# Attention and two MLPs on one core: transpositions in a PSUM bank of their own over two heads, and weight conversion without a shift

## The chip, the cores and the metric

The kernel runs on one core of one Trainium2 chip. The metric is the device time of one execution in microseconds (us), the median of several runs. TensorE (PE in the profile; PEld is its weight load), VectorE (DVE), ScalarE (ACT), GpSimd (POOL) and the queue of transfers (SP) each work through their own list of instructions in order, and wait for one another by semaphores. Matmul results land in PSUM, which has eight banks of 128 partitions x 512 float32.

## The reference, cut to what matters

```python
q, k, v: (4, 8, 576, 64) float32
q_rot, k_rot = (rotate(q), rotate(k))                 # rotary embedding over the 576 positions
scores = q_rot @ k_rot.T / sqrt(64)
attn   = exp(scores - max(scores, -1)); attn /= sum(attn, -1) + 1e-9
x      = (attn @ v) laid out as (2304 tokens, 512)
x      = (sigmoid(x @ w_gate) * (x @ w_val)) @ w_out  # 512 -> 1536 -> 512
h      = x @ w_in
out    = where(h > 0, h, exp(min(h, 0)) - 1) @ w_out2 # 512 -> 2048 -> 512
```

The weights of the MLPs are float64. Products are made at float32 accuracy from two parts, a rounded high part and the rest, so that each product is three matmuls in the MLPs and two in the scores.

## The kernel before, in words

**Attention.** There are 32 heads in 16 pairs. The work of a head is laid out in a *slot* of ten *steps* (`NSTEP`); step `h` of slot `i` issues one tile of scores of head `i` (`scores`, two matmuls K1xQ1 and K2xQ2 into a tile `s`, exponential on ACT into `e`), one tile of the row maxima of the head two slots later (`maxima`, one matmul into a tile `mt`, reduced by DVE into `MX`), and five steps late one product with V (`values`, tile `pv`). Steps 4 and 9 are the last score tile of each half, whose stationary has 64 columns instead of 128; their exponential is split in two, and DVE makes the low part `p` one and a half steps later (`low_part`). At step 0 DVE joins the maxima of the next head (`join`, `MJ`), and at step 1.5 PE turns them into a row (`max_row`, tile `mr` in the same pool as `mt`), which DVE copies (`row`) and a DMA takes into the operands `W`. An even head (the first of its pair) has ten `mt` beside it, an odd one eight.

**Preparing a pair.** POOL makes the rotary embedding of q and k (`rope_ops`; `rk`, `rt`, `rq`). `split` then transposes it on PE in four pieces, two for k and two for q (three, two, two and two 128x128 transpositions), into PSUM tiles `Tk_0`, `Tk_256`, `Tq_0`, `Tq_256`; for each piece ACT copies the rounded part into `hl` and DVE subtracts it for the rest. For pair `pr` all four pieces stand in slot `2*pr-4`, an even one, at steps 1.5 to 7.5. `move` sends the parts to `W` by DMA.

**PSUM in attention.** Eight banks: `ps_mt` has three (for `mt` and `mr`), `ps_qk` three (for `s` and for all transpositions), `ps_pv` two. A tile that finds no free bank makes PE wait for the reader of an earlier tile of its pool.

**Weights.** `split_w` converts float64 weights from their two 32-bit words, in pieces of 128x256, with seven DVE instructions (lines 121, 124, 126, 131, 134, 137, 140), one ACT copy (138) and two POOL instructions (141, 143). It is a generator; `pull` takes it one `yield` further. In attention one pull stands at step 2 and one at step 5 of each slot from 6 to 29, and each of them is one DVE instruction there. What is left of the first chunk's weights is pulled once a step from slot 30. In the MLPs the pulls are spread over the matmuls of the chunk before.

**MLPs.** Six chunks of the gated MLP and eight of the second (ELU) one, each for five blocks of up to 512 tokens; the second layer of a block runs one block behind the first. In the ELU chunks DVE also makes the activation (672, 673) and adds every output tile to `z` (730).

The order on each engine is the order in which the code is written; `at(slot, step, ...)` puts a call on an agenda that is emitted at that place.

Of the kernel before, what the change touches and what calls it, by code (L numbers as in the profile page):

```python
# [14 lines left out]
I32 = mybir.dt.int32  # L15
I64 = mybir.dt.int64


@with_exitstack
def attention_moe_moe_kernel(  # L20
# [81 lines left out]
    def split_w(c, n, half):  # L102
# [10 lines left out]
        for j in range(0, size, WP):  # L113
# [19 lines left out]

            nc.vector.tensor_single_scalar(e, low, 8, op=ALU.logical_shift_right)  # L134
            if c == 0:
                yield
            nc.vector.tensor_single_scalar(m, a.bitcast(I32), -0x00800000, op=ALU.bitwise_and)  # L137
            nc.scalar.copy(h, a)  # L138
            yield
            nc.vector.scalar_tensor_tensor(mf, in0=e, scalar=2.0**-44, in1=mf, op0=ALU.mult, op1=ALU.mult)  # L140
            nc.gpsimd.tensor_tensor(out=a, in0=a, in1=h.bitcast(F32), op=ALU.subtract)  # L141
# [44 lines left out]
    with ExitStack() as att:  # L186
# [9 lines left out]
        rope_p = prep.enter_context(tc.tile_pool(name="rope", bufs=1))  # L196
        ps_mt = banks.enter_context(tc.tile_pool(name="ps_mt", bufs=3, space=bass.MemoryType.PSUM))
        ps_qk = banks.enter_context(tc.tile_pool(name="ps_qk", bufs=3, space=bass.MemoryType.PSUM))
        ps_pv = banks.enter_context(tc.tile_pool(name="ps_pv", bufs=2, space=bass.MemoryType.PSUM))

# [119 lines left out]

        def split(pr, which, half, later=None):
# [6 lines left out]
            T = ps_qk.tile([P, 512], F32, tag="qk", name=f"T{which}{pr}_{c0}")[:, 0:n]  # L328
            rows = [rot[pr, which][:, c // P] for c in range(c0, c0 + HM, P)] + ([rot[pr, "t"]] if tails else [])
            for j, r in enumerate(rows):  # L330
                nc.tensor.transpose(T[:, j * P : (j + 1) * P], r.rearrange("p h d -> p (h d)"), ident)
            c0 += 0 if which == "k" else S + TL
            hi, lo = (parts[pr][:, 2 * j : 2 * j + 2].rearrange("p w s -> p (w s)")[:, c0 : c0 + n] for j in range(2))
            nc.scalar.copy(hi, T)
            rest = lambda: nc.vector.tensor_tensor(out=lo, in0=T, in1=hi.bitcast(F32), op=ALU.subtract)
            if later is None:
                rest()
            else:
                at(*later, rest)

# [82 lines left out]
        def scores(i, h):  # L423

            a, t = divmod(h, ST + 1)
            n = P if t < ST else TL
            if t == ST:

                p = probs[i, h] = p_p.tile([P, HA], F32R, tag="pt", name=f"p{i}_{h}")[:, 0:HS]
            else:  # L430
                e = probs[i, h] = e_p.tile([P, HA], F32, tag="ef", name=f"e{i}_{h}", bufs=2 * ST)[:, 0:HS]
            s = ps_qk.tile([P, 512], F32, tag="qk", name=f"s{i}_{h}")[0:n, 0:HS]
            for st, mv in (("K1", "Q1"), ("K2", "Q2")):
                nc.tensor.matmul(  # L434
                    s, lhsT=operand(i, st, t * P, n), rhs=operand(i, mv, a * HS, HS), start=st == "K1", stop=st == "K2"
                )
# [11 lines left out]
        def values(i, h):  # L448
# [9 lines left out]
            e = probs.pop((i, h))  # L458
            if t == ST:
                nc.tensor.matmul(out_ps[0:D], lhsT=VT[par][:, ab, 0:D], rhs=e, start=False, stop=False)  # L460
                nc.tensor.matmul(out_ps, lhsT=VT[par][:, ab, D : 3 * D], rhs=e, start=False, stop=True)
# [76 lines left out]
        for which in "kq":  # L538
            for half in range(2):
                at(-5, 1, split, 0, which, half)  # L540
            at(-5, 1, copies, 0, which, nc.vector.tensor_copy)
# [3 lines left out]
        for (which, half), st in zip((("k", 0), ("k", 1), ("q", 0), ("q", 1)), (10, 11, 17, 18)):  # L545
            at(-2, st, split, 1, which, half)
        at(-2, 13, copies, 1, "k", nc.scalar.copy)
# [3 lines left out]
        for pr in range(NPAIR):  # L551
            s0 = 2 * pr
            if pr > 1:
# [10 lines left out]
                for j, (which, half) in enumerate((("k", 0), ("k", 1), ("q", 0), ("q", 1))):  # L564
                    at(s0 - 4, (6.5, 7.5, 8.5, 9.5)[j] if pr == 2 else (1.5, 3.5, 5.5, 7.5)[j], split, pr, which, half, None if pr == 2 else (s0 - 4, 2.5 + 2 * j))
                at(s0 - 4, 10 if pr == 2 else 9, move, pr, 0)
                at(s0 - 4, 10 if pr == 2 else 9, last_queries, pr, nc.gpsimd.tensor_copy)
                at(s0 - 4, 19, move, pr, 1)
# [25 lines left out]
        at(5, 0, pull, gen)  # L594
        pulls = 14 * len(halves(0)) + 1
        early = [(slot, step) for slot in range(6, NHEAD - 2) for step in (2, 5)]
# [209 lines left out]
```

## Time and profile before

| what | us |
|---|---|
| median of 3 runs (lowest, highest) | 1164.22 (1162.93, 1165.01) |
| span of the profiled execution | 1164.2 |
| first score matmul of head 0 | 24.2 |
| first matmul of the first MLP | 319.7 |
| first matmul of the second MLP | 766.1 |
| end of the last matmul | 1159.6 |
| PE busy / DVE busy / POOL busy / ACT busy | 1138.5 / 937.7 / 605.0 / 451.2 |

The profile is that of one execution; its span and the median of the runs agree, so sums against the span are sums against the median. A *head* below is the stretch from one head's first score matmul to the next head's. PE is busy nearly all of the time, by a record in which the ends of pipelined matmuls are modelled, so what PE loses is read from the lengths of equal pieces of work (heads, chunks) and from the starts of matmuls, and not from the busy share. Instructions on DVE also overlap by a little: the next one starts before the row of the last one has ended.

### The profile page before, as it was taken

The page shows a single profiled execution, that of the slowest core. Times are in us where ns is not written, and L with a number is a line of the kernel's source. Part 1 is how long each engine was busy: PE and PEld are TensorE (multiplying, and loading weights), DVE is VectorE, ACT ScalarE, POOL GpSimd, SP SyncE. Part 2 cuts the span into 40 slices and gives each one's busy share as a digit, 9 for nine tenths or more (in the row PEclk, how much of TensorE's full clock was granted, in tenths as well). Part 3 has the DMA queues.
Part 4 walks back from the last instruction along what each step waited for, and adds up shares of the span by engine and source line. Part 5 has one row for each costly group of instructions (what it writes and reads, how often), then busy time and mean ns, then how long its engine had stood idle before and what let it go on. Part 6 is the DMA issues. An engine that isn't in the chain of part 4 may idle for free.

```text
span 1164.2 us, 16786 instructions
## 1 busy us (share of the span) xinstructions
PE 1138.5 (98%) x5728; PEld 960.5 (82%) x5728; DVE 937.7 (81%) x1994; ACT 451.2 (39%) x1037; POOL 605.0 (52%) x695
## 2 busy tenths in 40 slices
PE   5999999999999999999999999999999999999998
PEld 3888888888888888888888888888888888888887
DVE  6768888887876888667777766888999999999844
ACT  4666666667753321221222122344322222222221
POOL 8766666863343554434444435775554545545521
PEclk9999999999999999999999999999999999999999
DMA  6667677767121211111111110111111111110004
GB/s 166 158 161 184 163 179 169 163 158 160 41 94 37 73 55 40 52 37 47 44 38 54 37 55 19 37 37 37 55 37 55 37 37 55 37 55 1 1 37 127
DMA packets 58757, 88.03 MB, mean 76 GB/s; under 512 B 18176, under 2 KB 30736, under 8 KB 58672
## 3 DMA queue, kind: packets, MB, share of 16 engines
q1 hardware_dynamic: 58672, 86.96, 28.2%
q8 instruction: 45, 0.74, 0.3%
q14 instruction: 40, 0.33, 0.1%
HBM read 55.45 MB, written 4.87 MB: 52 GB/s over the span
## 4 chain that ended last, share of the span: by engine, by line
PE 78%; DVE 17%; ACT 2%; issue 1%; DMA 1%; SPq 0%; POOL 0%; POOLq 0%
PE h L647 12%; PE h L648 12%; PE h L649 12%; PE pv L463 9%; PE o L647 7%; PE o L648 7%; PE o L649 7%; PE s L434 7%; DVE z L730 3%; PE mt L387 3%; DVE g L673 2%; DVE g L672 2%; DVE ca L131 2%; DVE cm L140 1%; DVE MX L389 1%; DVE ce L134 1%
## 5 line engine op out<-in xcount | busy, mean ns | idle before, releaser
L679 POOL TENSOR_TENSOR gl<-g,gh 128x512 fp32r<-128x512 f32 (+1 forms) x140 | 168.6, 1204 | 330.2 <-ACT gh L678 261.7
L678 ACT CAST gh<-g 128x512 fp32r<-128x512 f32 (+1 forms) x140 | 81.0, 579 | 308.2 <-DVE g L673 171.1
L434 PE MATMUL s<-W 128*128 128x288 f32 (+1 forms) x640 | 182.0, 366 | 3.8 <-DVE p L444 1.3
L648 PE MATMUL h<-xl,wh 128*128 128x512 f32 (+1 forms) x480 | 176.6, 368 | 0.0
L647 PE MATMUL h<-xh,wh 128*128 128x512 f32 (+1 forms) x480 | 176.6, 368 | 0.0
L649 PE MATMUL h<-xh,wl 128*128 128x512 f32 (+1 forms) x480 | 176.5, 368 | 0.0
L463 PE MATMUL pv<-e,VF 128*128 128x288 f32 x512 | 166.0, 407 | 0.0
L141 POOL TENSOR_TENSOR ca<-ca,wh 128x256 f32<-128x256 f32 x136 | 111.5, 820 | 96.8 <-DVE cm L137 82.4
L389 DVE TENSOR_REDUCE MX<-mt 128x1 f32<-128x288 f32 x288 | 127.5, 450 | 40.9 <-PE mt L387 38.7
L434 PEld LDWEIGHTS s<-W 128*128 128x128 f32 (+1 forms) x640 | 106.1, 182 | 32.1 <-DVE p L444 5.2
L138 ACT CAST wh<-ca 128x256 fp32r<-128x256 f32 x136 | 55.1, 405 | 195.0 <-DVE ca L131 195.0
L143 POOL TENSOR_TENSOR wl<-ca,cm 128x256 fp32r<-128x256 f32 x136 | 111.0, 816 | 18.5 <-DVE cm L140 12.1
L441 ACT ACTIVATE e<-s 128x288 f32<-128x288 f32 x256 | 104.3, 411 | 41.4 <-PE s L434 38.2
L648 PE MATMUL h<-yl,wh 128*128 128x512 f32 (+1 forms) x320 | 117.7, 368 | 0.0
L649 PE MATMUL h<-yh,wl 128*128 128x512 f32 (+1 forms) x320 | 117.7, 368 | 0.0
L647 PE MATMUL h<-yh,wh 128*128 128x512 f32 (+1 forms) x320 | 117.7, 368 | 0.0
L668 DVE TENSOR_TENSOR g<-h,g 128x512 f32<-128x512 f32 (+1 forms) x60 | 38.2, 637 | 95.1 <-PE h L649 92.3
L647 PE MATMUL o<-wh,gh 128*128 128x512 f32 x288 | 112.7, 391 | 1.5 <-DVE z L730 1.2
L648 PE MATMUL o<-wl,gh 128*128 128x512 f32 x288 | 112.2, 389 | 0.0
L649 PE MATMUL o<-wh,gl 128*128 128x512 f32 x288 | 112.1, 389 | 0.0
L649 PEld LDWEIGHTS h<-xh,wl 128*128 128x128 f32 x480 | 90.5, 189 | 15.1
L647 PEld LDWEIGHTS h<-xh,wh 128*128 128x128 f32 x480 | 90.5, 189 | 15.0
(110 smaller groups left out, 2514.4 us busy)
## 6 DMA issues: line engine op xcount, KB each, us to landing
W<-hl SPq DMA_DIRECT2D x90, 288.0 KB
raw<-in_moe_w_out_dram SPq DMA_DIRECT2D x28, 512.0 KB
raw<-in_moe_w_in_dram SPq DMA_DIRECT2D x16, 512.0 KB
raw<-in_moe_w_gate_dram SPq DMA_DIRECT2D x12, 512.0 KB
raw<-in_moe_w_val_dram SPq DMA_DIRECT2D x12, 512.0 KB
rb<-d SPq DMA_DIRECT2D x32, 144.0 KB
k<-in_k_dram SPq DMA_DIRECT2D x16, 256.0 KB
q<-in_q_dram SPq DMA_DIRECT2D x16, 256.0 KB
```

The source lines that it names most:

```text
L138: nc.scalar.copy(h, a)
L141: nc.gpsimd.tensor_tensor(out=a, in0=a, in1=h.bitcast(F32), op=ALU.subtract)
L143: nc.gpsimd.tensor_tensor(out=l, in0=a, in1=mf, op=ALU.add)
L389: nc.vector.tensor_reduce(out=MX[pr % 2][:, a, c : c + 1], in_=m, axis=AX.X, op=ALU.max, negate=True)
L434: nc.tensor.matmul(s, lhsT=operand(i, st, t * P, n), rhs=operand(i, mv, a * HS, HS), start=st == "K1", stop=st == "K2")
L441: nc.scalar.activation(e, s, AF.Exp, scale=SCALE)
L463: nc.tensor.matmul(out_ps, lhsT=VF[par][:, ab, t], rhs=e, start=t == 0, stop=False)
L647: nc.tensor.matmul(ps, lhsT=ah, rhs=bh, start=j == 0, stop=False)
L648: nc.tensor.matmul(ps, lhsT=ah, rhs=bl, start=False, stop=False)
L649: nc.tensor.matmul(ps, lhsT=al, rhs=bh, start=False, stop=j == n - 1)
L678: nc.scalar.copy(hi, g)
L679: nc.gpsimd.tensor_tensor(out=lo, in0=g, in1=hi.bitcast(F32), op=ALU.subtract)
```

## The change

**Banks.** `ps_mt` has two banks instead of three. The freed bank is a pool `ps_t` for transpositions. For the first four pairs only the last piece of q of pairs 0 and 1 uses it; the rest stays in `ps_qk` as before.

**Order from the fifth pair on (`pr` >= 4).** The two k pieces move to slot `2*pr-5`, an odd one, and the two q pieces stay in slot `2*pr-4`; each is at step 4 or step 9, all in `ps_t`. The transpositions are no longer issued in a row: they are put on a list `between`, and `one_between` takes one of them ahead of each of the two score matmuls of that step (and the third of `Tk_256` ahead of the value product). The ACT copy follows behind the step, and DVE's subtraction one and a half steps behind it, except for `Tq_256`, where it follows at once. `move` and `last_queries` go from step 9 to step 10.

**Weights.** The shift of the low word by 8 bits (line 134 before) is gone; the last DVE instruction reads the low word itself as an unsigned number and multiplies by 2^-52 instead of 2^-44. For the first chunk each piece has six pulls instead of seven, so 12 fewer are left for slot 30 and later.

```diff
-            nc.vector.tensor_single_scalar(e, low, 8, op=ALU.logical_shift_right)
-            if c == 0:
-                yield
             nc.vector.tensor_single_scalar(m, a.bitcast(I32), -0x00800000, op=ALU.bitwise_and)
             nc.scalar.copy(h, a)
             yield
-            nc.vector.scalar_tensor_tensor(mf, in0=e, scalar=2.0**-44, in1=mf, op0=ALU.mult, op1=ALU.mult)
+            nc.vector.scalar_tensor_tensor(
+                mf, in0=low.bitcast(U32), scalar=2.0**-52, in1=mf, op0=ALU.mult, op1=ALU.mult
+            )
...
-        ps_mt = banks.enter_context(tc.tile_pool(name="ps_mt", bufs=3, space=bass.MemoryType.PSUM))
+        ps_mt = banks.enter_context(tc.tile_pool(name="ps_mt", bufs=2, space=bass.MemoryType.PSUM))
         ps_qk = banks.enter_context(tc.tile_pool(name="ps_qk", bufs=3, space=bass.MemoryType.PSUM))
+        ps_t = banks.enter_context(tc.tile_pool(name="ps_t", bufs=1, space=bass.MemoryType.PSUM))
...
+            for j, r in enumerate(rows):
+                if apart:
+                    between.append((turn, (j, r)))
+                else:
+                    turn(j, r)
+            if apart:
+                at(*apart, finish)
+            else:
+                finish()
...
+                    if pr < 4:
+                        at(s0 - 4, (6.5, 7.5, 8.5, 9.5)[j] if pr == 2 else (1.5, 3.5, 5.5, 7.5)[j], split, pr, which, half, ps_qk, "qk", None if pr == 2 else (s0 - 4, 2.5 + 2 * j))
+                    else:
+                        slot, step = s0 - 5 + j // 2, 4 + 5 * (j % 2)
+                        at(slot, step - 0.5, split, pr, which, half, ps_t, "t", (slot, step + 1.5) if j < 3 else None, (slot, step))
...
-        pulls = 14 * len(halves(0)) + 1
+        pulls = 12 * len(halves(0)) + 1
```

**What stands where.** On PE in an even head, before: the transpositions of one piece in a row, in the pool of the score tiles (`Tq_0` here).

```order
L387 MATMUL mt_5_2718<-W_161 128x288
L463 MATMUL pv_0_2721<-e_0_2627,VF_163 128x288
L331 MATMUL Tq_0_2728<-ident,rq_2528 128x128 x2
L434 MATMUL s_6_2735<-W_159 128x288 x2
L387 MATMUL mt_6_2739<-W_161 128x288
```

The same piece in the changed kernel, a step and a half earlier:

```order
L490 MATMUL pv_1_2654<-e_8_2622,VF_167 128x288
L337 MATMUL Tq_0_2706<-ident,rq_2533 128x128
L460 MATMUL s_4_2708<-W_162 64x288
L337 MATMUL Tq_0_2706<-ident,rq_2533 128x128
L460 MATMUL s_4_2708<-W_162 64x288
L411 MATMUL mt_4_2715<-W_164 128x288
```

Each transposition now has a score matmul of 64 stationary columns behind it.

On DVE at the start of that even head (`MX` reads `mt`, `MJ` joins the maxima, `p` is the low part of the head before), before:

```order
L389 TENSOR_REDUCE MX_168<-mt_0_2632 128x1
L394 TENSOR_REDUCE MJ_169<-MX_167 128x4
L444 TENSOR_TENSOR p_9_2616<-s_9_2617,p_9_2616 64x288
L389 TENSOR_REDUCE MX_168<-mt_1_2645 128x1
L477 COPY u_2494<-pv_0_2579 64x288
L411 CAST row_2655<-mr_2653 5x128
L389 TENSOR_REDUCE MX_168<-mt_2_2669 128x1
```

and in the changed kernel:

```order
L413 TENSOR_REDUCE MX_171<-mt_0_2651 128x1
L418 TENSOR_REDUCE MJ_172<-MX_170 128x4
L470 TENSOR_TENSOR p_9_2631<-s_9_2632,p_9_2631 64x288
L340 TENSOR_TENSOR hl_2569<-Tk_256_2630,hl_2569 128x384
L413 TENSOR_REDUCE MX_171<-mt_1_2665 128x1
L504 COPY u_2497<-pv_0_2593 64x288
L435 CAST row_2675<-mr_2673 5x128
L413 TENSOR_REDUCE MX_171<-mt_2_2684 128x1
```

The subtraction for `Tk_256`, of 384 columns, stands between `p` and the reduction of `mt_1`.

On DVE from the end of an even head into the odd one, before:

```order
L389 TENSOR_REDUCE MX_168<-mt_8_2767 128x1
L335 TENSOR_TENSOR hl_2659<-Tq_256_2758,hl_2659 128x256
L389 TENSOR_REDUCE MX_168<-mt_9_2778 128x1
L389 TENSOR_REDUCE MX_168<-mt_0_2799 128x1
L394 TENSOR_REDUCE MJ_170<-MX_168 128x5
L444 TENSOR_TENSOR p_9_2772<-s_9_2773,p_9_2772 64x288
L389 TENSOR_REDUCE MX_168<-mt_1_2813 128x1
```

and in the changed kernel:

```order
L413 TENSOR_REDUCE MX_171<-mt_8_2766 128x1
L413 TENSOR_REDUCE MX_171<-mt_9_2779 128x1
L340 TENSOR_TENSOR hl_2569<-Tq_256_2770,hl_2569 128x256
L413 TENSOR_REDUCE MX_171<-mt_0_2797 128x1
L418 TENSOR_REDUCE MJ_173<-MX_171 128x5
L470 TENSOR_TENSOR p_9_2771<-s_9_2772,p_9_2771 64x288
L413 TENSOR_REDUCE MX_171<-mt_1_2816 128x1
```

The subtraction for `Tq_256` has moved from before the last reduction of the even head to behind it, ahead of the first one of the odd head.

## Rows read from the trace of the kernel before

**Rows 1.** Busy time by windows, PE; each window is one even head, 4 to 26.
```profile
62.50:72.46 9.96, 9.68 (x63) 1.00 0.77 185
...
sum 123.63, PE 118.66; mean PE 9.89
```

**Rows 2.** The same view, all engines, odd heads 5 to 27: first and sum.
```profile
72.46:80.69 8.23, 8.23 (x51) 7.28 (x50) 5.70 (x15) 5.53 (x16) 7.70 (x11) 1.00 0.87 228
...
sum 99.25, PE 99.06 PEld 87.29 DVE 83.00 ACT 66.99 POOL 78.22; mean PE 8.25 PEld 7.27 DVE 6.92 ACT 5.58 POOL 6.52
```

**Rows 3.** The same view, head 28: an even head without transpositions.
```profile
285.38:293.85 8.47, 8.47 (x53) 7.52 (x52) 6.73 (x18) 5.61 (x15) 0.00 (x0) 1.00 0.63 141
```

**Rows 4.** Timeline of PE in head 26: start, length, what, [idle before].
```profile
271.05 0.38 PE L331 MATMUL Tk<-ident,rk 128*128 128x128 f32 x2
271.27 0.27 PE L331 MATMUL Tk<-ident,rt 128*128 128x128 f32 x1
...
273.36 0.41 PE L331 MATMUL Tq<-ident,rq 128*128 128x128 f32 x2 [0.29 <-ACT e L441]
```

**Rows 5.** Timeline of all engines in head 16, around a long conversion instruction.
```profile
180.07 1.28 POOL L316 TENSOR_TENSOR rk<-rk,sk 128x512 f32<-128x512 f32 x1
180.14 1.36 DVE L121 TENSOR_SCALAR ce<-raw 128x256 int32<-128x256 int32 x1
...
182.03 0.53 PE L434 MATMUL s<-W 128*128 128x288 f32 x2 [0.42 <-DVE p L444]
```

**Rows 6.** Timeline of all engines, start of head 28 (begins at 285.38).
```profile
286.53 0.45 DVE L444 TENSOR_TENSOR p<-s,p 64x288 fp32r<-64x288 f32 x1
...
286.91 0.44 DVE L389 TENSOR_REDUCE MX<-mt 128x1 f32<-128x288 f32 x1
...
287.37 0.19 PEld L387 LDWEIGHTS mt<-W 128*128 128x128 f32 x1
```

**Rows 7.** Timeline of all engines, start of head 27 (an odd one).
```profile
277.14 0.43 PE L434 MATMUL s<-W 128*128 128x288 f32 x2
277.25 0.39 ACT L441 ACTIVATE s<-s 64x288 f32<-64x288 f32 x1
...
277.74 0.46 DVE L389 TENSOR_REDUCE MX<-mt 128x1 f32<-128x288 f32 x1 [0.20 <-PE mt L387]
...
278.68 0.44 DVE L389 TENSOR_REDUCE MX<-mt 128x1 f32<-128x288 f32 x1
...
279.16 0.19 PEld L387 LDWEIGHTS mt<-W 128*128 128x128 f32 x1
```

**Rows 8.** Groups by line, DVE, heads 4 to 29: count, busy us, mean ns.
```profile
L335 DVE TENSOR_TENSOR hl<-Tk,hl 128x256 fp32r<-128x256 f32 (+1 forms) x24 | 11.5, 480 | 0.0
L335 DVE TENSOR_TENSOR hl<-Tq,hl 128x256 fp32r<-128x256 f32 x24 | 10.1, 420 | 0.3
```

**Rows 9.** Groups by line, whole span: the ACT copy of a piece.
```profile
L334 ACT CAST hl<-Tq 128x256 fp32r<-128x256 f32 x32 | 11.8, 372 | 14.1 <-PE Tq L331 13.9
```

**Rows 10.** Timeline of all engines in the prologue, the first ten maxima.
```profile
13.94 2.90 PE L387 MATMUL mt<-W 128*128 128x288 f32 x7 [2.96 <-DVE W L361]
...
14.56 1.98 DVE L389 TENSOR_REDUCE MX<-mt 128x1 f32<-128x288 f32 x5 [0.76 <-PE mt L387]
...
15.07 1.45 PEld L387 LDWEIGHTS mt<-W 128*128 128x128 f32 x4 [0.42 <-DVE MX L389]
```

**Rows 11.** Timeline of DVE in the prologue, the second set of maxima.
```profile
21.90 2.34 DVE L389 TENSOR_REDUCE MX<-mt 128x1 f32<-128x288 f32 x6
```

**Rows 12.** Busy time by windows: ELU chunk 1, and chunks 2 to 5 together.
```profile
812.66:861.80 49.14, 49.14 (x230) 41.16 (x228) 46.82 (x93) 15.16 (x33) 26.07 (x28) 1.00 0.13 43
861.80:1061.14 199.34, 197.87 (x914) 164.38 (x913) 187.73 (x382) 53.57 (x112) 100.06 (x106) 1.00 0.14 43
```

**Rows 13.** Groups by line, DVE, ELU chunks 2 to 5.
```profile
L140 DVE SCALAR_TENSOR_TENSOR cm<-ce,cm 128x256 f32<-128x256 int32 x33 | 19.3, 586 | 0.2
L126 DVE SCALAR_TENSOR_TENSOR cm<-raw,cm 128x256 int32<-128x256 int32 x33 | 17.2, 521 | 0.2
...
L134 DVE TENSOR_SCALAR ce<-raw 128x256 int32<-128x256 int32 x32 | 14.7, 460 | 0.2
```

The window rows have the columns: window, its length, busy time of PE, PEld, DVE, ACT and POOL with the count of instructions (of PE alone in rows 1), the granted clock of TensorE as a share, the share of the DMA engines that was busy, and GB/s.

More of the change, by code (lines that the diff above doesn't have):

```diff
@@ L16 @@
 I64 = mybir.dt.int64
+U32 = mybir.dt.uint32
 @with_exitstack
@@ L319, in attention_moe_moe_kernel, with split @@
         parts = {}
-        def split(pr, which, half, later=None):
+        between = []
+        def split(pr, which, half, pool, tag, later=None, apart=False):
             if which == "k" and half == 0:
@@ L327, in split, with turn, rest, finish @@
             c0, n = half * HM, HM + (P if tails else 0)
-            T = ps_qk.tile([P, 512], F32, tag="qk", name=f"T{which}{pr}_{c0}")[:, 0:n]
+            T = pool.tile([P, 512], F32, tag=tag, name=f"T{which}{pr}_{c0}")[:, 0:n]
             rows = [rot[pr, which][:, c // P] for c in range(c0, c0 + HM, P)] + ([rot[pr, "t"]] if tails else [])
-            for j, r in enumerate(rows):
-                nc.tensor.transpose(T[:, j * P : (j + 1) * P], r.rearrange("p h d -> p (h d)"), ident)
             c0 += 0 if which == "k" else S + TL
             hi, lo = (parts[pr][:, 2 * j : 2 * j + 2].rearrange("p w s -> p (w s)")[:, c0 : c0 + n] for j in range(2))
[L334 to L337, printed above, removed]
-            else:
-                at(*later, rest)
+            def turn(j, r):
+                nc.tensor.transpose(T[:, j * P : (j + 1) * P], r.rearrange("p h d -> p (h d)"), ident)
+            def rest():
+                nc.vector.tensor_tensor(out=lo, in0=T, in1=hi.bitcast(F32), op=ALU.subtract)
+            def finish():
+                assert not between
+                nc.scalar.copy(hi, T)
+                if later is None:
+                    rest()
+                else:
+                    at(*later, rest)
+            for j, r in enumerate(rows):
[5 more added lines that the diff above has]
+                at(*apart, finish)
+            else:
+                finish()
+        def one_between():
+            if between:
+                fn, args = between.pop(0)
+                fn(*args)
         def move(pr, ab):
@@ L433, in scores @@
             for st, mv in (("K1", "Q1"), ("K2", "Q2")):
+                if t == ST:
+                    one_between()
                 nc.tensor.matmul(
@@ L539, in attention_moe_moe_kernel @@
             for half in range(2):
-                at(-5, 1, split, 0, which, half)
+                at(-5, 1, split, 0, which, half, *((ps_t, "t") if (which, half) == ("q", 1) else (ps_qk, "qk")))
             at(-5, 1, copies, 0, which, nc.vector.tensor_copy)
@@ L545, in attention_moe_moe_kernel @@
         for (which, half), st in zip((("k", 0), ("k", 1), ("q", 0), ("q", 1)), (10, 11, 17, 18)):
-            at(-2, st, split, 1, which, half)
+            at(-2, st, split, 1, which, half, *((ps_t, "t") if (which, half) == ("q", 1) else (ps_qk, "qk")))
         at(-2, 13, copies, 1, "k", nc.scalar.copy)
@@ L564, in attention_moe_moe_kernel @@
                 for j, (which, half) in enumerate((("k", 0), ("k", 1), ("q", 0), ("q", 1))):
-                    at(s0 - 4, (6.5, 7.5, 8.5, 9.5)[j] if pr == 2 else (1.5, 3.5, 5.5, 7.5)[j], split, pr, which, half, None if pr == 2 else (s0 - 4, 2.5 + 2 * j))
-                at(s0 - 4, 10 if pr == 2 else 9, move, pr, 0)
-                at(s0 - 4, 10 if pr == 2 else 9, last_queries, pr, nc.gpsimd.tensor_copy)
+                    if pr < 4:
[3 more added lines that the diff above has]
+                        at(slot, step - 0.5, split, pr, which, half, ps_t, "t", (slot, step + 1.5) if j < 3 else None, (slot, step))
+                at(s0 - 4, 10 if pr == 2 or pr > 3 else 9, move, pr, 0)
+                at(s0 - 4, 10 if pr == 2 or pr > 3 else 9, last_queries, pr, nc.gpsimd.tensor_copy)
                 at(s0 - 4, 19, move, pr, 1)
```

1 line of the change is left out of this document (added).

## The prediction

> **What bounds the kernel now.** I read the windows first, cut where equal pieces of work begin. An odd head of attention takes 8.23 us wherever nothing disturbs it, and twelve of them take 99.25 [rows 2], which is 0.49 over twelve times 8.23. An even head without transpositions takes 8.47 [rows 3]. The twelve even heads with transpositions take 123.63 [rows 1], 22.0 over twelve times 8.47. An ELU chunk takes 49.14 where PE runs through [rows 12], and chunks 2 to 5 together 199.34, which is 2.8 over four times that. PE is thus the bound, and what any change off PE can gain is these excesses: 22.5 us in the heads from 4 to 27 and 2.8 in the ELU chunks. The reader is to see that repeating pieces have a floor, and that the excess over it is all that waits cost.
>
> Then I read the timeline of PE in an even head, to split the 22.5 into work and waiting. Three transpositions start at 271.05 and, the third, at 271.27 [rows 4]: 0.11 us each. Nine a pair in twelve pairs are 108, so 11.9 us is PE's own work, and 10.6 us is waiting. The wait that comes back in every pair is that of `Tq_0` for a score tile's exponential [rows 4]: it shares three banks with the score tiles, which transpositions hold until DVE has read them. The first even head of the set took 9.96 [rows 1], 1.49 over 8.47, and its nine transpositions are 0.99 of it; so the recurring wait is 0.5 a pair, 6.0 in all. The other 4.6 is irregular: a conversion instruction of 1.36 us on DVE, beside a POOL instruction of 1.28, holds back the low part `p`, and PE waits 0.42 for it [rows 5].
>
> **Transpositions, their own bank.** All nine are still issued, with the same shape, so PE's 11.9 us stay. With a bank to themselves the recurring wait for a score tile goes: -6.0. The irregular waits come from DVE being late, and DVE has as many instructions per pair as before; moving two of the four subtractions into the odd head evens them out. I take half of the 4.6 as gone: -2.3, with 0 and -4.6 as bounds. Step 4 or 9 holds the bank for some steps, and the next piece comes five steps later (over 4 us), while copy and subtraction take 0.37 and 0.42 to 0.48 [rows 8, 9]; I cost the single bank at nothing. The k pieces need their rotary embedding some seven steps earlier than before; POOL makes it in slot `2*pr-6`, a slot ahead, and I cost that at nothing too; POOL is busy 6.5 of 8.25 us in an odd head [rows 2], so it can slip a little without being late. The DMAs of `move` are issued a step later and have most of a head until the first `mt` that reads them.
>
> **Two banks for the maxima, even heads.** `mt_0`, `mt_1`, `mr` and `mt_2` now take two banks in turn, so the load for `mt_2` waits until DVE has reduced `mt_1`. In head 28, which has no transpositions, that reduction starts at 286.91 right behind `p`, ends at 287.35, and the load of `mt_2` starts at 287.37 [rows 6]: two banks would just do there. The change puts the subtraction for `Tk_256` between `p` and this reduction. It takes 0.48 on the mean [rows 8], so the reduction ends at 287.83; a released load starts 0.05 after the reduction (in the prologue the first reduction starts at 14.56 and the load follows at 15.07 [rows 10]; with 0.46 for the reduction [rows 7] 0.05 is left). The load comes at 287.88 instead of 287.37: 0.51 us that PE stands still, since scores and value products are queued behind this `mt` on PE.
>
> **Two banks, odd heads.** The subtraction for `Tq_256` now stands ahead of the odd head's first reduction, and it needs ACT's copy, which stands behind the two exponentials of the last step. In head 27 the second of these runs from 277.25 to 277.64 [rows 7]; the copy, 0.37 [rows 9], ends at 278.02, and the subtraction, 0.42 [rows 8], at 278.44. The first reduction, at 277.74 before, starts at about 278.39 (instructions on DVE overlap by some 0.05): 0.65 later, and all that follows it is as late, since DVE goes from one to the next there. The reduction of `mt_1` moves from 278.68 to 279.33 and ends at 279.77; the load of `mt_2` comes at 279.82 instead of 279.16 [rows 7]: 0.66 us. The row `mr` waits for the joined maxima on the way, inside this figure. So 1.17 a pair, in twelve pairs +14.0. Were DVE to overlap more, or the copy to come earlier, 0.8 a pair would stay (+9.6); that is the lower bound, and +14.0 is what I take.
>
> **Prologue.** The first ten `mt` go to DVE one after the other with little else, five reductions in 1.98 us, 0.38 each [rows 10]. With two banks a reduction frees the bank of the next but one: 0.46 of reduction, 0.05 until the load, and at least 0.62 from a matmul's start to its reduction (13.94 to 14.56), 1.13 for two, 0.565 each. Eight of the ten pay 0.185: +1.5. The six reductions of the second set (2.34 us, 0.39 each [rows 11]) feed the transpositions of q behind them on PE; five pay as much: +0.9. Nothing else is going on in the prologue that would hide it: the scores of head 0 wait for these transpositions. I take +2.4, between +1.2 and +3.0.
>
> **Weights.** Each piece loses one DVE instruction, 0.46 us in the ELU chunks [rows 13], and its last one reads raw words, as L126 does (0.52), instead of a dense tile as L140 did (0.59): no dearer by the nearest row [rows 13]. With some eight pieces a chunk DVE gets 3.7 us back of the 46.9 it is busy in one (187.73 over four) [rows 12]. The excess there is 0.7 a chunk. I take 2.6 of the 2.8 as gained, with 0 and 2.8 as bounds. In the gated chunks and in attention the instruction is hidden: the number of pulls per head is the same, so DVE has as many conversions per head as before.
>
> **Sum.** -6.0 - 2.3 + 14.0 + 2.4 - 2.6 = +5.5 on the profiled span of 1164.2, which is the median of the runs as well: **1169.7 us**. The bounds of this case: -10.6 + 9.6 + 1.2 - 2.8 = -2.6 gives 1161.6, and -6.0 + 14.0 + 3.0 = +11.0 gives 1175.2.
>
> **Rivals.** *Two banks are enough* (the other side). All 10.6 us of waits go and none comes: DVE would have to reduce `mt_1` before the load of `mt_2` in every head. With +1.5 in the prologue and -2.6 in the ELU chunks the time is 1152.5. For it: in head 28 the reduction does end before the load [rows 6]. Against: by 0.02 us only, and what is put ahead of it takes 0.48. It decides at that point: if the subtraction is done while DVE idles, this case holds.
>
> *Transpositions become cheaper between score matmuls.* If 0.11 is the time to load the next stationary and not that of the pass, a score matmul before each one hides the load. A score matmul of 288 columns occupies PE for about 0.13 (two of them from 277.14 to the next `mt` are 0.27 in this trace), so 128 columns are 0.06, and 108 times 0.05 is 5.4: 1164.3. Against: the third transposition, in front of a load of 64 columns, and the second, in front of one of 128, are equally long as far as I can read the starts. The Trainium skill, TensorE: Matmul & The Clock Gate, section "Back-to-back issue gap", has the isolated gap as N/2.4 + 2.5 ns, 56 ns for 128 columns; the trace has 0.11 [rows 4], so by that rule this rival would be the case and the sum would be 1164 or so. The measurement decides for me.
>
> *Half the waits.* The new waits are real but half as long, because DVE catches up inside the step: 14.0 becomes 7.0, and the time 1162.7.
>
> *Two banks let every long conversion through to PE.* Such an instruction (1.36 us [rows 5]) delays a reduction by almost a microsecond; with three banks an odd head shows nothing of it [rows 2], with two it could cost 0.5 each time. A third of the 48 pulls would make 8 us more, and the time 1178.
>
> **Chances.** My sum 0.64, of which 0.10 lies within 0.2%; two banks are enough 0.15; cheaper transpositions 0.08; half the waits 0.06; long conversions 0.07. Within 0.2%, 2.3 us, is about what a measurement of this kernel can tell from no change, so faster is below 1161.9 and slower above 1166.5. Faster: 0.15 and 0.02 of the halved waits, 0.17. Same: 0.10 + 0.08 + 0.04 = 0.22. Slower: 0.54 + 0.07 = 0.61. The range from 1161 to 1176 leaves out the first rival and most of the last, 0.2 together.
>
> **What would show it.** In the profile of the changed kernel: no wait of a transposition for an exponential; PE waiting at `mt` for a reduction near the third `mt` of nearly every head from 5 to 27; even heads near 9.4 us and odd ones near 9.4 (8.23 + 0.55 + 0.66); the scores of head 0 starting 2 us later; ELU chunks all near 49.2. It would be wrong if odd heads with k pieces took 8.8 (their floor with five transpositions), if the first score matmul stayed at 24.2, or if ELU chunks kept their excess.

## The result, and the profile after

The changed kernel takes 1175.37 us (median, 1174.72 to 1177.22), the kernel before 1163.58 beside it: 1.0102 of it, 95% interval 1.0088 to 1.0117. The forecast was slower, 1169.7 with a range to 1176; the sign and the main place (heads 4 to 27) were right, and the loss is about twice the forecast one.

The profiled span is 1175.4, 11.2 over the one of before. A span stands some 1.8 below the time of its execution (1175.4 and 1177.22 here). So the two agree less well than was said ahead of the prediction: the span of before, 1164.2, belongs by that to an execution of about 1166.0 (an estimate), and both profiles are some 2 us longer than their kernel's median. Differences of spans can be set against differences of medians even so (11.2 and 11.8). Cut where equal pieces of work begin, as before (first score matmul of a head, first matmul of a chunk):

| stretch | before | after | difference | forecast |
|---|---|---|---|---|
| to the first scores of head 0 | 24.24 | 26.03 | +1.79 | +2.4 |
| head 0 | 11.70 | 12.88 | +1.18 | 0 |
| heads 1 to 3 | 26.56 | 27.28 | +0.72 | 0 |
| heads 4 to 27 | 222.88 | 230.62 | +7.74 | +5.7 |
| heads 28 to 31 and on to the MLP | 34.35 | 36.91 | +2.56 | 0 |
| gated MLP | 446.33 | 446.33 | 0 | 0 |
| ELU MLP | 393.52 | 390.74 | -2.78 | -2.6 |

These are rows of busy time by windows of the changed kernel: head 3, head 22 (even), head 23 (odd), heads 4 to 27, heads 28 to 31, the ELU MLP. The columns are those of [rows 2].

```profile
57.40:66.19 8.79, 8.79 (x56) 7.85 (x55) 6.06 (x17) 5.92 (x17) 6.50 (x9) 1.00 0.55 112
240.44:249.94 9.50, 9.18 (x57) 8.01 (x56) 7.59 (x20) 6.16 (x17) 4.80 (x6) 1.00 0.78 193
249.94:259.43 9.49, 9.29 (x57) 7.80 (x56) 7.79 (x20) 6.50 (x19) 7.24 (x10) 1.00 0.65 153
66.19:296.81 230.62, 222.09 (x1305) 189.18 (x1304) 181.46 (x463) 149.98 (x403) 146.78 (x193) 1.00 0.68 164
296.81:333.72 36.91, 34.37 (x193) 28.69 (x192) 30.14 (x73) 25.91 (x68) 11.46 (x16) 1.00 0.24 57
780.05:1170.79 390.74, 390.74 (x1825) 327.67 (x1823) 330.09 (x617) 117.02 (x236) 187.94 (x194) 1.00 0.14 44
```

The same view of the kernel before, for the last three:

```profile
62.50:285.38 222.88, 217.72 (x1311) 186.56 (x1309) 186.89 (x464) 152.16 (x403) 144.88 (x191) 1.00 0.71 169
285.38:319.73 34.35, 34.20 (x193) 28.59 (x192) 28.67 (x75) 26.17 (x68) 10.52 (x15) 1.00 0.24 60
766.06:1159.58 393.52, 392.05 (x1825) 327.23 (x1823) 342.65 (x671) 114.21 (x236) 187.43 (x194) 1.00 0.14 43
```

Head 3 is the cleanest piece: it now holds the five transpositions of k of the fifth pair (0.55 of the 0.72 in the table), no wait of PE stands in it, and it takes 8.79 where an undisturbed odd head takes 8.23 [rows 2]. A transposition ahead of a score matmul thus costs 0.11 us, as three in a row did [rows 4]. With that, head 23 has 8.23 + 5 x 0.11 = 8.78 of work and 0.7 of waiting, head 22 has 8.47 + 4 x 0.11 = 8.91 and 0.6.

Who waited for whom on PE, one row each, first of the kernel before, then of the changed one (us in total, times, longest):

```profile
PE Tq L331 <- ACT e L441: 2.3, 9, 0.3
```
```profile
PE mt L411 <- DVE MX L413: 9.5, 34, 0.5
```

The wait of `Tq_0` for a score tile's exponential [rows 4] has no row any more; `mt` waits for a reduction instead, 34 times: 27 of them, 7.7 us, in heads 4 to 27, and seven, 1.8 us, ahead of head 0 and in it. Timeline of the changed kernel at the start of head 22 (compare [rows 6]):

```profile
241.59 0.45 DVE L470 TENSOR_TENSOR p<-s,p 64x288 fp32r<-64x288 f32 x1
...
242.07 0.56 DVE L340 TENSOR_TENSOR hl<-Tk,hl 128x384 fp32r<-128x384 f32 x1
...
242.54 0.45 DVE L413 TENSOR_REDUCE MX<-mt 128x1 f32<-128x288 f32 x1
...
243.04 0.19 PEld L411 LDWEIGHTS mt<-W 128*128 128x128 f32 x1 [0.55 <-DVE MX L413]
```

and at the start of head 23 (compare [rows 7]):

```profile
250.11 0.39 ACT L467 ACTIVATE s<-s 64x288 f32<-64x288 f32 x1
...
250.51 0.37 ACT L344 CAST hl<-Tq 128x256 fp32r<-128x256 f32 x1
...
250.92 0.42 DVE L340 TENSOR_TENSOR hl<-Tq,hl 128x256 fp32r<-128x256 f32 x1 [0.59 <-ACT hl L344]
...
251.26 0.45 DVE L413 TENSOR_REDUCE MX<-mt 128x1 f32<-128x288 f32 x1
...
251.83 0.19 PEld L433 LDWEIGHTS mr<-identr,MJ 128*128 128x128 f32 x1 [0.41 <-DVE MJ L418]
...
252.18 0.44 DVE L413 TENSOR_REDUCE MX<-mt 128x1 f32<-128x288 f32 x1
...
252.68 0.19 PEld L411 LDWEIGHTS mt<-W 128*128 128x128 f32 x1 [0.43 <-DVE MX L413]
```

In both the chain is the forecast one: subtraction, reduction of the second maximum, load for the third, 0.05 us behind its end.

### The profile page after: what moved, and what is told of

Read it like the earlier page. It is cut to its first block, busy times and chain, and to the rows that moved or that the text cites. A ratio compares the mean times of both kernels' runs of the same rounds, so it can differ in the third digit from the quotient of the medians.

```text
span 1175.4 us, 16735 instructions
## 1 busy us (share of the span) xinstructions
PE 1144.8 (97%) x5728; PEld 965.2 (82%) x5728; DVE 898.7 (76%) x1858; ACT 452.0 (38%) x1037; POOL 605.7 (52%) x695
## 4 chain that ended last, share of the span: by engine, by line
PE 91%; DVE 5%; ACT 2%; issue 1%; DMA 1%; SPq 0%; POOL 0%; DVEq 0%; POOLq 0%; ACTq 0%
PE h L680 14%; PE h L678 14%; PE h L679 14%; PE o L678 10%; PE o L679 10%; PE o L680 10%; PE pv L490 8%; PE s L460 6%; PE mt L411 4%; DVE MX L413 2%; DVE p L470 1%; DVE hl L340 1%; PE Tk L337 1%; PE Tq L337 1%; PE pv L488 1%
## 5 line engine op out<-in xcount | busy, mean ns | idle before, releaser
L460 PE MATMUL s<-W 128*128 128x288 f32 (+1 forms) x640 | 185.7, 370 | 4.6 <-ACT e L467 2.3
L460 PEld LDWEIGHTS s<-W 128*128 128x128 f32 (+1 forms) x640 | 109.2, 182 | 30.8 <-ACT e L467 3.9
L679 PEld LDWEIGHTS h<-xl,wh 128*128 128x128 f32 x480 | 90.5, 189 | 15.0
```

Source lines behind the costliest of these rows:

```text
L460: nc.tensor.matmul(s, lhsT=operand(i, st, t * P, n), rhs=operand(i, mv, a * HS, HS), start=st == "K1", stop=st == "K2")
L679: nc.tensor.matmul(ps, lhsT=ah, rhs=bl, start=False, stop=False)
```

## The experiments

**The two parts alone.** `weights_only` is the kernel before with the weight part of the change:

```diff
-            nc.vector.tensor_single_scalar(e, low, 8, op=ALU.logical_shift_right)
-            if c == 0:
-                yield
...
-        pulls = 14 * len(halves(0)) + 1
+        pulls = 12 * len(halves(0)) + 1
```

> The kernel before with the weight part alone: no shift, raw low word times 2^-52, 12 pulls for each half of the first chunk instead of 14; banks and transpositions as before. My theory: the ELU stretch gains what it gained in the changed kernel, 2.8 us (393.5 to 390.7), and heads 4 to 27 keep 222.9; the stretch from head 28 to the first MLP also loses what it lost there, 2.6 us (34.35 to 36.9), because ACT's rounding copy of a piece now follows DVE's scaling by one pull instead of two, stands waiting in ACT's queue, and the exponentials behind it wait too. Together about 1164.0. Rival: the 2.6 us come from the banks or from a later start of these heads; then heads 28 to 31 take 34.35 and the kernel takes 1161.4.

Measured: 1165.67 us, 1.0015 of the kernel before (1.0006 to 1.0025). Heads 4 to 27, heads 28 to 31, the ELU MLP:

```profile
60.98:283.88 222.90, 217.41 (x1310) 186.72 (x1309) 185.17 (x464) 152.41 (x404) 146.15 (x193) 1.00 0.71 169
283.88:320.61 36.73, 34.26 (x194) 28.64 (x193) 30.03 (x73) 25.86 (x68) 11.43 (x16) 1.00 0.24 56
766.93:1157.67 390.74, 390.74 (x1825) 327.56 (x1823) 329.35 (x616) 117.38 (x236) 187.89 (x194) 1.00 0.14 44
```

The weight part gains its 2.8 us in the ELU chunks and loses 2.4 in the last four heads; the rival falls. The median is 1.7 over the expected 1164.0; the profiled execution is one of the shorter ones (1164.11), so the trace does not show where this lies. `banks_only` is the changed kernel with the shift and 14 pulls put back:

```diff
+            nc.vector.tensor_single_scalar(e, low, 8, op=ALU.logical_shift_right)
+            if c == 0:
+                yield
...
-        pulls = 12 * len(halves(0)) + 1
+        pulls = 14 * len(halves(0)) + 1
```

> The changed kernel with the shift back (14 pulls for each half): the bank and transposition part alone. My theory: heads 4 to 27 take the 230.6 us of the changed kernel, the prologue and heads 0 to 3 are 3.7 us later than before, heads 28 to 31 take 34.35 as before and the ELU stretch 393.5 as before: 1164.2 + 7.7 + 3.7 = 1175.6. Rival of above, that the 2.6 us at heads 28 to 31 belong to the banks: 1178.2.

Measured: 1174.95 us, 1.0093 (1.008 to 1.0106). Heads 4 to 27, and heads 28 to 31:

```profile
65.39:293.89 228.50, 221.23 (x1306) 188.89 (x1305) 178.51 (x463) 149.46 (x402) 145.96 (x191) 1.00 0.69 165
293.89:328.37 34.48, 34.33 (x193) 28.63 (x192) 28.75 (x73) 26.23 (x68) 10.26 (x15) 1.00 0.25 61
```

Nearly the whole loss is that of the banks and the order, and heads 28 to 31 are whole again. One number was not expected: heads 4 to 27 take 228.5 here and 230.6 with the weights changed too. The 2.1 lie in heads 8, 14 and 20, which take 10.22 to 10.23 in the changed kernel and 9.48 to 9.53 here. They are six slots apart, and six slots of two pulls are the 12 pulls of one half: so with 12 pulls an instruction of a half comes back at the same place six slots later. The last conversion of a piece (line 138) falls beside POOL's rotary embedding in these three heads and takes 1.19 to 1.21 us; in `banks_only`, with 14 pulls, no conversion of more than 0.7 us falls in them. `weights_only`, with 12 pulls and three banks, has long ones in the same heads (0.84 to 1.53 on line 138). Timeline of the changed kernel in head 8:

```profile
111.02 1.27 POOL L317 TENSOR_TENSOR rk<-rk,sk 128x512 f32<-128x512 f32 x1
...
111.36 1.21 DVE L138 SCALAR_TENSOR_TENSOR cm<-raw,cm 128x256 f32<-128x256 uint32 x1
...
112.60 0.45 DVE L470 TENSOR_TENSOR p<-s,p 64x288 fp32r<-64x288 f32 x1
...
113.43 0.45 DVE L413 TENSOR_REDUCE MX<-mt 128x1 f32<-128x288 f32 x1
...
113.93 0.40 PE L411 MATMUL mt<-hl,QT 128*128 128x288 f32 x1 [0.47 <-DVE MX L413]
```

**Two banks with nothing else.** `two_banks` is the kernel before with

```diff
-        ps_mt = banks.enter_context(tc.tile_pool(name="ps_mt", bufs=3, space=bass.MemoryType.PSUM))
+        ps_mt = banks.enter_context(tc.tile_pool(name="ps_mt", bufs=2, space=bass.MemoryType.PSUM))
```

> The kernel before with two banks for the maxima instead of three and nothing else; the eighth bank stays empty. My theory, that the waits come from the subtractions put ahead of the reductions and not from two banks by themselves: odd heads stay at 8.23 to 8.3, even heads at 9.9 to 10.5, and only the prologue and head 0 pay, 1.8 and up to 1.2 us: 1166 to 1168. Rival, two banks by themselves make PE wait in every head: odd heads near 8.7 to 8.9, even ones 10.4 and more, 1175 or later.

Measured: 1168.84 us, 1.0034 (1.0022 to 1.0046). Head 5, and heads 4 to 27:

```profile
73.40:81.65 8.25, 8.25 (x51) 7.30 (x50) 5.71 (x15) 5.54 (x16) 7.70 (x11) 1.00 0.90 228
```
```profile
63.50:285.76 222.26, 218.04 (x1310) 187.14 (x1309) 185.43 (x464) 152.13 (x403) 144.77 (x191) 1.00 0.72 170
```

The heads stay as they were; what this trace shows lost lies ahead of head 0, whose scores start at 26.06, and in head 0 (last section). The median is 0.8 over the expected range; the profiled execution is the fastest of the five (1166.45), so the rest of the loss isn't seen in it. Two banks are enough for the maxima so long as DVE has nothing between `p` and the second reduction.

**The subtractions put later.** `late_both` is the changed kernel with all its banks; it moves only DVE's two subtractions, and with them the pair's transfers:

```diff
-                        at(slot, step - 0.5, split, pr, which, half, ps_t, "t", (slot, step + 1.5) if j < 3 else None, (slot, step))
-                at(s0 - 4, 10 if pr == 2 or pr > 3 else 9, move, pr, 0)
+                        at(slot, step - 0.5, split, pr, which, half, ps_t, "t", (slot, step + 3.5) if j == 1 else (slot, step + 1.5) if j < 3 else (slot, step + 3.5), (slot, step))
+                at(s0 - 4, 13 if pr > 3 else 10 if pr == 2 else 9, move, pr, 0)
```

> The changed kernel with the subtractions for Tk_256 and Tq_256 two steps and three and a half steps later, both behind the reduction of the third maximum of a head; the transfers of a pair three steps later. All banks stay. My theory: the waits of 0.59 and 0.66 us at the third maximum go, even heads take 8.95, odd ones 8.8 with their five transpositions (about 0.11 us each), so 24 heads take 14 us less: 1161 to 1163. Rival, two banks are the cause whatever DVE does ahead: the waits stay in place, 1173 or more. Second rival, the subtraction only moves the wait to a later maximum: half of it stays, 1168.

Measured: 1184.78 us, 1.0178 (1.0165 to 1.0191): slower than either kernel. The first rival left room for such a time, but the wait that it named is gone; none of the three said what came instead. The list of waits on PE:

```profile
PE mt L411 <- DMA W<-hl: 7.3, 7, 1.6
...
PE Tq L337 <- DVE hl L340: 6.0, 11, 1.3
PE Tk L337 <- DVE hl L340: 4.3, 7, 0.9
...
PE mt L411 <- DVE MX L413: 1.8, 7, 0.5
```

The old wait did go, from 9.5 to 1.8, and the 1.8 all lie before head 4. Two others came. The next piece's transpositions want the single bank, and DVE reaches the subtraction only behind a conversion instruction, as in head 25 (DVE, then PE):

```profile
278.87 1.14 DVE L127 SCALAR_TENSOR_TENSOR cm<-raw,cm 128x256 int32<-128x256 int32 x1
279.94 0.41 DVE L340 TENSOR_TENSOR hl<-Tq,hl 128x256 fp32r<-128x256 f32 x1
```
```profile
280.49 0.30 PE L337 MATMUL Tk<-ident,rk 128*128 128x128 f32 x1 [0.76 <-DVE hl L340]
```

And the transfers, three steps later, are late for the first maximum of the pair. So the single bank, which the prediction costed at nothing, is free only while the subtraction is early, as it is in the changed kernel, and the transfers have little to spare.

`behind_second_both` moves less: both subtractions directly behind the second reduction, the transfers right behind that of q.

```diff
+                if apart and (which, half) == ("q", 1):
+                    move(pr, 0)
...
+                        at(slot, step - 0.5, split, pr, which, half, ps_t, "t", (slot, step + 2) if j % 2 else (slot, step + 1.5), (slot, step))
...
```

> The changed kernel with the subtractions for Tk_256 and Tq_256 half a step and two steps later, directly behind the reduction of the second maximum of a head and its companion copy, ahead of the copy of the row; the transfers of the pair follow the subtraction at once. Theory: the two subtractions standing ahead of the second reduction are the whole of the wait at the third maximum, and late_both failed by other waits, since it put them behind a conversion instruction and so close to the next piece's transpositions in the single bank, and its transfers three steps late. Then step 2 takes 0.72 again, even heads take 8.95, odd ones 8.8, heads 4 to 27 together some 14 us less than 230.6, and the time is 1161 to 1163. Rival: the work that DVE has between the first maximum and the fourth is too much for two banks wherever the subtraction stands, and the wait goes to the fourth maximum, whose bank the row copy frees: 1168 or more.

Measured: 1168.04 us, 1.0039 (1.0028 to 1.0051): the lower end of the rival's range, and not the 1161 to 1163 of the theory. Heads 4 to 27:

```profile
65.98:287.68 221.70, 218.34 (x1306) 189.83 (x1305) 183.32 (x463) 150.30 (x403) 147.79 (x193) 1.00 0.72 170
```

8.9 us of the 230.6 are gone. The wait at the third maximum went, as the theory said, and a part of it came back at the fourth, as the rival said. Odd heads take 8.86 to 8.89 where undisturbed, a tenth over their floor; even ones 9.26 to 9.33, since 0.36 of the wait has moved to the fourth maximum: it takes the bank of `mr`, and the row copy stands behind the subtraction (lines of this kernel are two higher):

```profile
254.33 0.56 DVE L340 TENSOR_TENSOR hl<-Tk,hl 128x384 fp32r<-128x384 f32 x1
...
254.81 0.27 DVE L437 CAST row<-mr 5x128 fp32r<-5x128 f32 x1
...
255.13 0.40 PE L413 MATMUL mt<-W 128*128 128x288 f32 x1
```

`behind_second_k` has the first half of that edit alone:

```diff
+                        at(slot, step - 0.5, split, pr, which, half, ps_t, "t", (slot, step + 2) if j == 1 else (slot, step + 1.5) if j < 3 else None, (slot, step))
```

> Of the kernel just named only the move of the subtraction for Tk_256; that for Tq_256 stands as in the changed kernel. Theory: only the twelve even heads gain, 0.5 to 0.6 us each, odd heads stay at 9.43 to 9.49: 1168 to 1170. Rival, odd and even waits depend on one another, because a head that is late is late for the next: both change or neither.

Measured: 1174.46 us, 1.0092 (1.0077 to 1.0106), 4.5 us over the top of the expected range, mostly because of that moved wait (0.36 in each of twelve heads). Odd heads stay at 9.39 to 9.48 and even ones fall to 9.26 to 9.41 where undisturbed; so even and odd waits are separate, each from its own subtraction.

**The lost cover in heads 28 to 31.** `weights_padded` is `weights_only` with an empty pull where the shift was:

```diff
-            nc.vector.tensor_single_scalar(e, low, 8, op=ALU.logical_shift_right)
             if c == 0:
                 yield
...
```

> The kernel before without the shift, but with an empty pull in its place, so that the first chunk's halves keep 14 pulls and every other instruction of attention its step. Theory: heads 28 to 31 and the way to the first MLP stay at 34.35 us, the ELU stretch falls by 2.8 us: 1161.2. Rival: the last instruction of a piece, on raw words, costs more than the one on a dense tile and DVE is late in heads 30 and 31 in any case: 36.7 there and 1164.

Measured: 1160.89 us, 0.9976 of the kernel before (0.9967 to 0.9984), as expected, and the only kernel here that is faster clear of noise. The ELU MLP takes 390.74, and heads 28 to 31:

```profile
285.71:319.62 33.91, 33.81 (x193) 28.65 (x192) 27.73 (x69) 26.22 (x68) 10.10 (x15) 1.00 0.25 62
```

The timeline of the changed kernel in head 30 shows what the pull had covered:

```profile
318.65 0.41 DVE L132 SCALAR_TENSOR_TENSOR ca<-ce,cm 128x256 f32<-128x256 int32 x1
319.09 0.40 ACT L136 CAST wh<-ca 128x256 fp32r<-128x256 f32 x1 [0.94 <-DVE ca L132]
...
319.40 0.40 ACT L467 ACTIVATE e<-s 128x288 f32<-128x288 f32 x1
...
319.86 0.53 PE L460 MATMUL s<-W 128*128 128x288 f32 x2 [0.76 <-ACT e L467]
...
320.34 0.69 DVE L172 TENSOR_TENSOR xl<-x,xh 128x512 fp32r<-128x512 f32 x1 [0.96 <-ACT xh L171]
```

ACT's rounding copy follows DVE's scaling by one pull, at one pull a step. DVE is busy with `xl`, so ACT stands 0.94 for `ca`, the exponential behind it is late, PE waits 0.76; then DVE waits 0.96 for ACT, and so on. With the empty pull the copy comes a step later and finds `ca` done. The same two instructions in head 30 of `weights_padded`:

```profile
307.75 0.42 DVE L132 SCALAR_TENSOR_TENSOR ca<-ce,cm 128x256 f32<-128x256 int32 x1
...
308.58 0.40 ACT L138 CAST wh<-ca 128x256 fp32r<-128x256 f32 x1
```

The empty pull also puts every later pull of the chunk elsewhere, which this run does not separate from the distance; the chain above speaks for the distance. In every kernel with 12 pulls a half head 30 takes 8.98 or 8.99, in every one with 14 it takes 7.70 or 7.71.

**Both repairs.** `behind_second_padded` joins `behind_second_both` and the empty pull.

```diff
+            if c == 0:
+                yield
...
-        pulls = 12 * len(halves(0)) + 1
+        pulls = 14 * len(halves(0)) + 1
```

> The first of these kernels with the empty pull of the third. If both reasons hold and add, heads 4 to 27 take 216 to 217, heads 28 to 31 take 34.4, the ELU stretch 390.7: 1158 to 1160.5, less than either kernel. If the waits of DVE add in other ways, 1162 or more.

Measured: 1164.24 us, 1.0005 (0.9996 to 1.0014), over the 1158 to 1160.5 that the theory gave. Heads 28 to 31 take 34.0, heads 4 to 27 take 220.35: the empty pull gives back what was expected, the wait at the fourth maximum not. `behind_row_padded` puts both subtractions behind the row copy (the diff is against that kernel, as the next one):

```diff
-                        at(slot, step - 0.5, split, pr, which, half, ps_t, "t", (slot, step + 2) if j % 2 else (slot, step + 1.5), (slot, step))
+                        at(slot, step - 0.5, split, pr, which, half, ps_t, "t", (slot, step + 2.5) if j % 2 else (slot, step + 1.5), (slot, step))
```

> As behind_second_padded, but each of the two subtractions half a step later still, behind the copy of the row. Theory: what was left of the wait was that the fourth maximum takes the bank of mr, which the row copy frees, and that copy stood behind the subtraction; now the fourth maximum starts in time, step 3 of an even head goes from 1.48 to 1.13 and that of an odd one from 1.22 to 1.12, heads 4 to 27 fall from 220.3 to about 215, and the time is 1159 to 1160. Rival: the reduction of the third maximum is now behind the subtraction, and the fifth maximum waits for it in the same way: heads at 9.28 and 8.86 as before, 1164.

Measured: 1169.57 us, 1.0047 (1.0033 to 1.0062), over both expectations. Odd heads reach 8.75 to 8.80 where undisturbed, their floor, so the bank of `mr` was the rest of the wait and the fifth maximum does not take it over. Even heads lose more than that at their first maximum, since the pair's transfers now stand behind the row's in SP's queue (waits on PE in heads 4 to 27):

```profile
PE mt L415 <- DMA W<-hl: 5.7, 9, 0.9
```

`mixed_padded` puts the subtraction of k behind the row copy and leaves that of q ahead of it:

```diff
-                        at(slot, step - 0.5, split, pr, which, half, ps_t, "t", (slot, step + 2) if j % 2 else (slot, step + 1.5), (slot, step))
+                        at(slot, step - 0.5, split, pr, which, half, ps_t, "t", (slot, step + (1.5, 2.5, 1.5, 2)[j]), (slot, step))
```

> The subtraction for Tk_256 behind the copy of the row, that for Tq_256 behind the second maximum and ahead of the row, with the pair's transfers right behind it; the empty pull as before. Theory: the even head loses its wait at the fourth maximum (step 3 at 1.13) and pays no wait for transfers at step 0 (0.66), since these are no later than in behind_second_padded; the odd head keeps 0.10. Heads 4 to 27 then take 12 x 8.95 + 12 x 8.87 and 2 to 3 us of irregular waits, about 216, and the time is 4 us under that of behind_second_padded: 1159.5 to 1161. Rival: the transfers are late whenever the heads get shorter, since they then have less time: the even heads pay 0.3 to 0.7 at step 0 and the time stays at 1164.

Measured: 1162.87 us, 0.999 (0.9979 to 1.0001). Heads 4 to 27:

```profile
65.62:283.43 217.81, 215.25 (x1306) 189.67 (x1304) 180.93 (x457) 149.79 (x402) 145.48 (x191) 1.00 0.72 172
```

Even heads take 8.89 and odd ones 8.86 where nothing irregular happens, 5.1 us less in all than before the change, or 4.5 with the 0.55 that now stands in head 3. In this stretch the bank with its order does pay, then, once DVE's order fits the two banks; the way to the first scores takes 2.4 of it back. For the whole kernel a gain is not shown: the interval holds 1, and the time lies between the expectation and its rival. Against `weights_padded`, whose median is lower, the order is not settled: they ran beside different runs of the kernel before, and their times overlap (1160.64 to 1164.95 and 1158.82 to 1163.11).

**The new order without the bank.** `order_only` is the changed kernel with three banks for the maxima and all transpositions in the banks of the scores:

```diff
-        ps_mt = banks.enter_context(tc.tile_pool(name="ps_mt", bufs=2, space=bass.MemoryType.PSUM))
+        ps_mt = banks.enter_context(tc.tile_pool(name="ps_mt", bufs=3, space=bass.MemoryType.PSUM))
...
-        ps_t = banks.enter_context(tc.tile_pool(name="ps_t", bufs=1, space=bass.MemoryType.PSUM))
...
```

> The changed kernel with the banks of the kernel before: three for the maxima, and all transpositions in the three banks of the score tiles; the order over two heads, the interleaving and the weights as changed. Theory: the waits at the third maximum go, but each piece now keeps a score tile's bank until DVE's subtraction one and a half steps later, so the second score tile behind each piece waits for that, 0.4 to 0.9 us four times a pair: 1180 to 1205. So the new order needs the bank. Rival: the three banks of the scores have room enough, as before the change, and the maxima's third bank was all that was missing: 1162 to 1166.

Measured: 1181.33 us, 1.0146 (1.0122 to 1.017). The size is as expected, the wait is not quite the one named:

```profile
PE s L459 <- ACT e L466: 14.2, 50, 1.4
```

The piece and the half's last score tile hold two of the three banks, so each score tile behind them takes turns with the one just before it and waits for that one's exponential, not for the subtraction. The order needs the bank.

## Why the prediction was right, and where it was not

- **The recurring wait of 6.0 goes**: right in size. Where nothing else waits, an even head and the 0.55 that went to the odd one take 8.89 + 0.55 = 9.44 in `mixed_padded`, against 9.90 to 9.96 before: about 0.5 a pair. The row of the wait that the prediction named is gone, but it held only 2.3 of the 6.0; what the rest waited for, and whether the bank or the interleaving took it away, no run separates.
- **The nine transpositions cost as much as before**: right; head 3 has 0.56 for five. The rival of cheaper transpositions falls. The Trainium skill, TensorE: Matmul & The Clock Gate, section "Back-to-back issue gap", has an isolated gap of N/2.4 + 2.5 ns, which it says under-counts at small N; by that formula five of 128 columns would be 0.28 us, an estimate. The trace does not agree, with its 0.56, and the measurement decides.
- **Even heads +6.1**: the mechanism right, shown by `two_banks` and `behind_second_k`; measured 0.59 each, 7.1. The mis-sized term is the subtraction for `Tk_256`. I took the mean of its group, 0.48 [rows 8], but that row says "+1 forms": the piece of 384 columns takes 0.56.
- **Odd heads +7.9**: right in path and size: undisturbed ones take 9.40 to 9.49 over their 8.78, and head 27, which has no transpositions, 8.93 over 8.23: 0.67 on the mean, 8.0 in twelve. Part of it falls at `mr`, which waits 0.41 for the joined maxima, and the rest at the third maximum.
- **Prologue +2.4**: right. Five pairs of reductions start every 1.16 us (the rows below; 1.13 forecast), so ten take 5.52 instead of 3.94, and the second six 3.1 instead of 2.34 [rows 10, 11]: +2.4. From the first reduction to the first scores it is 9.68 to 9.69 us in the four kernels with three banks for the maxima and 12.05 to 12.07 in the nine with two. The scores of head 0 come only 1.79 later because the first reduction came 0.6 earlier in this trace. That start scatters from 13.95 to 14.85 over the traces, with three banks as with two; why, I did not follow.

```profile
13.95 0.82 DVE L413 TENSOR_REDUCE MX<-mt 128x1 f32<-128x288 f32 x2 [0.76 <-PE mt L411]
...
15.11 0.82 DVE L413 TENSOR_REDUCE MX<-mt 128x1 f32<-128x288 f32 x2 [0.34 <-PE mt L411]
```

- **Half of the irregular 4.6 goes**: wrong in size. What is left over from 230.62 after the terms above (222.88 - 6.0 + 7.1 + 8.0, and 0.55 less because five transpositions now stand in head 3) is -0.8, not -2.3. Heads 8, 14 and 20 carry 2.1 of what stayed, by the meeting of the weight conversion with POOL that `banks_only` does not have. The rival of long conversions was this mechanism, at three pulls instead of sixteen.
- **ELU chunks -2.6**: right, -2.78; no row of PE waiting is left there. One term of the working was too large: DVE's busy time in chunks 2 to 5 falls from 187.73 [rows 12] to 182.33, 1.35 a chunk and not 3.7. The rows of its instructions overlap, so one that is removed gives back less than its length. What it gave was still more than the excess of 0.7 a chunk.
- **"In attention the instruction is hidden: the number of pulls per head is the same"**: wrong, and the largest miss, +2.56. The count was the wrong thing to look at. The removed instruction had a pull of its own, and that pull was the distance between DVE's scaling and ACT's copy. In heads 30 and 31, at one pull a step, this distance was needed.
- **Two banks are enough** (the rival on the other side): true without subtractions in the way, false with them, as its own point of decision said.

The forecast of +5.5 and the measured +11.2 of the spans differ by the 2.6 of heads 28 to 31, 1.5 of irregular waits, 1.1 of larger new waits, 1.2 of head 0 and 0.2 of heads 1 to 3, less 0.6 in the prologue and 0.2 in the ELU chunks. Of the 1.2 some 0.5 belongs to the two banks (last section); the rest of it and the 0.6 are scatter between executions.

## What to carry to other kernels

A pool's last spare buffer is worth what its reader does between two releases: before taking it, list the instructions that stand ahead of that reader on its engine, after the change. An instruction taken out of a step-wise schedule takes its step along, and whatever waited behind that step must be looked for on the other engines, where the schedule is densest. And a group's mean with "+ forms" is not the duration of the shape on the path.

## What was not expected of the hardware

**Half speed in head 0.** Four kernels that run the same code up to the end of head 0 with three banks take 11.70, 10.24, 12.14 and 10.23 us for it. PE stood idle for 1.2 to 1.5 us before the same six score matmuls in each; but for the first, they then start 0.24 us apart in two of the kernels, and 288 columns in 0.24 us are 1.2 per ns, as at 1.2 GHz. In the other two they start 0.13 apart (the last 0.20), near the rate of 2.4 GHz. The column of the granted clock reads 1.00 in all. First the kernel before, then `order_only`:

```profile
27.83 1.81 PE L434 MATMUL s<-W 128*128 128x288 f32 x6 [1.18 <-ACT e L441]
```
```profile
27.33 1.12 PE L459 MATMUL s<-W 128*128 128x288 f32 x6 [1.36 <-ACT e L466]
```

`two_banks` runs them in 1.13, the changed kernel at the slow rate. At the full rate head 0 takes 10.72 and 10.73 in the two kernels with two banks that ran so (`behind_row_padded`, `two_banks`) and 10.23 and 10.24 in the two with three: 0.5 of head 0 is the two banks'. The rest is scatter: this part of a single span differs by up to 2 us between kernels with the same code, and a difference of that size is to be read from the medians. What decides it stays open.

**A neighbour on POOL stretches a DVE instruction.** The conversion instructions of one shape take 0.27 to 0.43 us in heads 4 to 27 when POOL is idle, and up to 1.5 beside POOL, mostly beside its rotary embedding ([rows 5], and 1.21 in head 8 above). Some beside POOL stay at 0.27, and why is open. Which of them are long changes with the rhythm, 12 or 14 pulls against two a slot: the changed kernel's last instruction of a piece (line 138) averages 1.02 us there, over seven, and 0.53 in the ELU chunks.
